# Where the softmax sums and their spread reciprocals are turned: TensorE matmuls before, VectorE 32x32 block turns after

## The chip, the core and the metric

The kernel runs on one core of a Trainium2 chip. A core has five engines with a queue of instructions each: PE (TensorE, matrix products; its weight loads are shown as PEld), DVE (VectorE), ACT (ScalarE), POOL (GpSimd) and SP (SyncE, which here only issues DMAs). The metric is the device time of one launch in microseconds (us), as the median of several runs. The profile is of one execution of its own.

## The reference, cut to what matters

Two independent heads read separate inputs, and their outputs are put side by side. Head A is a long convolution (a state space kernel `K` from complex exponentials, then an FFT convolution of length 4096 over 448 channels). Head B is plain attention over 2048 positions with 16 heads of 28 columns:

```
qkv = (x @ wqkv) ...           # B_x [1, 2048, 448]
scores = einsum("bhqd,bhkd->bhqk", q, k) * 28 ** -0.5
p = softmax(scores, axis=-1)
o = einsum("bhqk,bhkd->bhqd", p, v)
b = o.transpose(...).reshape(B, S, D) @ wo
out = concatenate([a, b], axis=-1)
```

The change lies in the division of the softmax: `o` is computed without it, and each column of `o` is then multiplied by the reciprocal of its row sum.

## The kernel before, in words

**Stages.** The first 228 us or so prepare both heads (projections, seeds of the exponentials). Then comes the attention, with most of head A laid into its gaps. The attention works by *units*: 4 groups `g` of 4 heads times 4 chunks `c` of 512 queries, 16 units numbered 0 to 15. A unit has 16 steps, one for each 128 keys, so the main loop (lines 1061 to 1118) has 256 steps `s`. Units 0 to 11 end while the powers of head A are still being formed on POOL and DVE; the last of these belong to step 200 or so. After that come the spectra and the final products of head A.

**One step.** The order of the instructions is written out by hand, and on each engine the instructions run in the order in which the program issues them (line 919):

```
ORDER = ('m0', 's0', 'm1', 's1', 'v', 'f', 'pv', 'f', 'v', 'k', 'm2', 's2', 'm3', 's3', 'v')
```

- `s0` to `s3` (`s_mm`, line 769): the scores of one head, a PE product into the PSUM tile `pss`, then ACT's exponential `p`.
- `m0` to `m3` (`max_mm`, line 189): part of the row maxima of a unit 19 steps ahead. Each takes a PSUM tile `pm`. `m0` is read by ACT (`rl`), `m1` by DVE (`rl`, which also waits for ACT's `rl`), `m2` and `m3` by DVE reductions (`mx`). From step 237 on there is none of these.
- `v` (`vec`, line 1056): one DVE piece of head A's powers (`g`, `zg`), if any is queued.
- `pv` (`pv_step`, line 776): the products of `p` and `v` into the PSUM tile `po`, summed over the 16 steps. A column of ones stands at index 28 (`DH`) of each head's 32 columns of `v`, so row 28 of each 32 rows of `po` holds the softmax sum.
- `f`: a *slot* (`slot`, line 1012). It runs at most one piece: the queue `urgent` first, then the output projections `p_due`, then `m_due` (three PE pieces for each block of head A), then `u_due` (its FFT pieces, until about step 100), then the spectra and final products (`f_slot`). From step 238 on there is a third slot at the end of each step (line 1109). After the last step, slots follow one another until nothing is left (line 1122).

**The ring.** The pieces and the maxima take their PSUM tile by `w_tile` (line 127): three tiles in turn, whoever asks. Whoever asks for the fourth waits until the readers of the first are done. From about step 200 on it is four tiles of one name.

**The end of a unit** (`fin`, line 789). It is called right after the unit's last `pv`. ACT copies `po` to SBUF as `o` (128 rows: 4 heads of 32; 512 queries). Two closures are queued:

- `sums`, two slots later: 16 small PE products (each is two matmul records in the trace) pick the four sums of each query out of `o` with the constant `sel`, and lay them with the queries on the partitions, 16 columns for each partition. DVE takes the reciprocal `r`, ACT spreads it over 32 columns each (`rb`, 128x512).
- `scale`, four slots after the unit's end: 16 PE products turn `rb` back with `ident`, and DVE multiplies: `on = o * pm`. For groups 0 to 2 `on` goes to DRAM. For the last group, units 12 to 15, four projections (`project`, line 815) follow, of 16 PE products each, whose first 12 read the stored groups (`og`) and whose last 4 read `on`.

Both closures ask the ring for a tile, and both use up a slot of `urgent`, so that the slot's other queues move on by one slot. Head A's final products (`one`, line 901) use a constant `wb`, which `finish` loads when the first of them is due.

Of the kernel before, what the change touches and what calls it, by code (L numbers as in the profile page):

```python
# [8 lines left out]
F32 = mybir.dt.float32  # L9
# [9 lines left out]
D = 448  # L19
# [73 lines left out]
def body(ctx, tc, a, out):  # L93
# [23 lines left out]
    const = pool(ctx, "const")  # L117
    ident = const.tile([128, 128], F32, name="ident")
    nc.sync.dma_start(ident, a["ident"])
    sel = const.tile([128, HG], F32, name="sel")  # L120
    kones = const.tile([128, 1], F32, name="kones")
    w1 = const.tile([128, 2, 128], F32, name="w1")

# [3 lines left out]
    def w_tile():  # L127

        n_ring[0] += 1
        return ps_w[0].tile([128, CQ], F32, name=f"pm{n_ring[0] % ps_w[1]}")  # L130
# [7 lines left out]
    def mm32(o, w, x_, start, stop, at=0):  # L138

        for i in range(w.shape[-1] // 32):  # L140
            c = slice(32 * i, 32 * i + 32)
            nc.tensor.matmul(o[c], w[:, c], x_, start=start, stop=stop, tile_position=(0, at + 32 * i))
# [85 lines left out]
    with ExitStack() as st:  # L228
# [89 lines left out]
        pw2 = s_p.tile([128, LV], F32, name="pw2")  # L318
        nc.sync.dma_start(pw2, a["pw2"])
        nc.sync.dma_start(kones, a["kones"])  # L320
        nc.sync.dma_start(sel, a["sel"])
        nc.sync.dma_start(w1, a["w1"])
        def split_w(s):
            for k in range(NCK):
# [464 lines left out]
    def fin(u, s_):  # L789
        g, c = divmod(u, NQ)  # L790
        o = kq_p.tile([128, CQ], F32, name="o")
        nc.scalar.activation(o, o_u[u], AF.Copy)
        on = kq_p.tile([128, CQ], F32, name="on", bufs=2)
        rb = kq_p.tile([128, 4, HG, 32], F32, name="rb")
        og = og_u.pop(u, None)

        def sums():
            pw = w_tile()
            for t in range(4):
                mm32(pw[:, t * HG:(t + 1) * HG], o[:, t * 128:(t + 1) * 128], sel, start=True, stop=True)  # L800
            r = kq_p.tile([128, 4, HG], F32, name="r", bufs=2)
            nc.vector.reciprocal(r, pw[:, :4 * HG].rearrange("p (t h) -> p t h", h=HG))
            nc.scalar.activation(rb, r[:, :, :, None].to_broadcast([128, 4, HG, 32]), AF.Copy)

        def scale():
            pw = w_tile()
            for t in range(4):
                mm32(pw[:, t * 128:(t + 1) * 128], rb[:, t].rearrange("p h e -> p (h e)"), ident, True, True)
            nc.vector.tensor_tensor(on, o, pw, ALU.mult)
            if g < G - 1:  # L810
                nc.sync.dma_start(on_d[c][g], on)
            else:
                p_due.extend((s_ + PD + PS * t, lambda t=t: project(t)) for t in range(4))

        def project(t):
            pw = w_tile()
            ts = slice(t * 128, (t + 1) * 128)
            for g2 in range(G):
                mm32(pw[:, :D], og[:, g2, ts] if g2 < G - 1 else on[:, ts], wo_t[g2 // 2][:, g2 % 2, :],
                     start=g2 == 0, stop=g2 == G - 1)  # L820
            y = kq_p.tile([128, D], F32, name="y", bufs=2)
            nc.scalar.activation(y, pw[:, :D], AF.Copy)
            q0 = c * CQ + t * 128
            nc.sync.dma_start(out[q0:q0 + 128, D:], y)

        soon_slot(UG[1], sums)
        soon_slot(UG[2], scale)

    fk = {}

# [43 lines left out]
    def finish(f, qc, p, ps, bufs=(2, 2)):  # L874

        t_ = {}

        def rows(t, m, i, n):

            w = t.ap[0][0]  # L880
            return bass.AP(tensor=t.tensor, offset=t.offset + (16 * m + 4 * qc + i) * w + f * DF,
                           ap=[[32 * w, 64], [w, n], [1, DF]])

        def load():
            t_["zi"] = p.tile([128, 4, 2, DF], F32, name="zi", bufs=bufs[0])
            nc.sync.dma_start(t_["zi"], z_d[f].rearrange("(q m h c) k d -> (h c k) q m d", m=2, h=2, c=2)
                              [:, qc * 4:qc * 4 + 4])
            t_["u"] = p.tile([128, 4, DF], F32, name="ut", bufs=2)
            for m in range(2):
                nc.sync.dma_start(t_["u"][64 * m:64 * m + 64], rows(u_a, m, 0, 4))  # L890
            if "dsk" not in fk:
                fk["dsk"], fk["wb"] = p.tile([128, D], F32, name="dsk"), p.tile([128, 64], F32, name="wb")
                t = a["A_D_skip"]
                nc.sync.dma_start(fk["dsk"], bass.AP(tensor=t.tensor, offset=t.offset, ap=[[0, 128], [1, D]]))
                nc.sync.dma_start(fk["wb"], a["wb"])

        def skip():
            nc.gpsimd.tensor_tensor(t_["u"], t_["u"],
                                    fk["dsk"][:, None, f * DF:(f + 1) * DF].to_broadcast([128, 4, DF]), ALU.mult)

        def one(i):
            if i == 0:
                t_["ot"] = p.tile([128, 4, DF], F32, name="ot", bufs=bufs[1])
            pf = ps()[:, :DF]
            for m in range(2):
                mm32(pf[64 * m:64 * m + 64, :], fk["wb"], t_["zi"][:, i, m, :], True, True, 64 * m)
            ot = t_["ot"]
            jbi = lambda t, o_: t.rearrange(o_ + " -> p j b i", j=4, i=2)
            nc.vector.tensor_tensor(jbi(ot[:, i], "p (j b i)"), jbi(pf, "p (b j i)"), jbi(t_["u"][:, i], "p (j b i)"), ALU.add)
            if i % 2:  # L910
                for m in range(2):
                    nc.sync.dma_start(rows(out, m, i - 1, 2), ot[64 * m:64 * m + 64, i - 1:i + 1])
        return load, [(0, lambda i=i: one(i)) for i in range(4)], skip
# [11 lines left out]
    k_seeds(0)  # L925
    k_seeds(0)

    urgent, back = collections.deque(), collections.deque()
    powers = {"g": collections.deque(), "e": collections.deque()}
    done = {"mm": -1}  # L930
    u_jobs = [u_stage1(q) for q in range(16)] + [u_stage2(m) for m in range(16)]
# [73 lines left out]
    def soon_slot(gap, f):  # L1005
        n_urgent[0] += 1
        urgent.append((n_slot[0] + gap, n_urgent[0], f))
        q = sorted(urgent)
        urgent.clear()
        urgent.extend(q)  # L1010

    def slot(s_):
        n_slot[0] += 1
        if urgent and urgent[0][0] <= n_slot[0]:
            urgent.popleft()[2]()
        elif s_ >= NS and f_slot(s_, "s"):
            pass
        elif p_due and p_due[0][0] <= s_:
            p_due.popleft()[1]()
        elif m_due and m_due[0][0] <= s_:  # L1020
            m_due.popleft()[1]()
        elif u_due and u_due[0][0] <= s_:
            u_part(*u_due.popleft()[1:])
        else:
            f_slot(s_, "s") or f_slot(s_, "f")
# [93 lines left out]
    pv_step(*prev)  # L1119
    fin(prev[0], NS)  # L1120
    s = NS
    while urgent or p_due or m_due or u_due or any(q[k] for q in (f_jobs, f_tasks, f_loaded) for k in "sf"):
        slot(s)
        s += 0.5
    assert not k_due and not powers["g"] and not powers["e"]
# [4 lines left out]
def constants():  # L1130
    import numpy as np
    k = {}
    k["ident"] = np.eye(128)
    sel, ones = np.zeros((128, HG)), np.zeros((128, 1))
    for j in range(HG):
        sel[32 * j + DH, j] = 1.0
        ones[32 * j + DH:32 * j + DH + 2] = 1.0
    k["sel"], k["kones"] = sel, ones
    k["pw2"] = np.tile(2.0 ** np.arange(LV), (128, 1))
    n1, k1 = np.arange(N1), np.arange(N1)  # L1140
    n2, k2 = np.arange(N2), np.arange(N2)
    th = 2 * np.pi * np.outer(n1, k1 + 0.25) / N1
    w1 = np.zeros((2, 128, 128))
    wb = np.zeros((2, 2, N1, 2, N1))
    for j in range(4):
        w1[0, 32 * j:32 * j + 32, 32 * j:32 * j + 32] = np.cos(th)
        w1[1, 32 * j:32 * j + 32, 32 * j:32 * j + 32] = np.sin(th)
    for h in range(2):
        wb[h, 0, :, h, :] = np.cos(th).T / L
        wb[h, 1, :, h, :] = np.sin(th).T / L  # L1150
    k["w1"] = w1.transpose(1, 0, 2)
    k["wb"] = wb.transpose(0, 1, 2, 4, 3).reshape(128, N2)
    ph = 2 * np.pi * ((k1[:, None, None] + 0.25) * n2[None, :, None] / L + n2[None, :, None] * k2[None, None, :] / N2)
    c, s = np.cos(ph).transpose(1, 0, 2), np.sin(ph).transpose(1, 0, 2)
    m2 = np.zeros((2, N2, N1, 2, 64))
    m2[0, :, :, 0], m2[0, :, :, 1] = c, s
    m2[1, :, :, 0], m2[1, :, :, 1] = -s, c
    k["m2u"] = m2.reshape(2, 16, 4, N1, 128).transpose(1, 0, 2, 3, 4).reshape(128, N1, 128)
    wa = np.zeros((2, 64, N1, N2, 2))
    ct, st = c.transpose(2, 1, 0), s.transpose(2, 1, 0)  # L1160
    wa[0, ..., 0], wa[0, ..., 1] = ct, -st
    wa[1, ..., 0], wa[1, ..., 1] = st, ct

    wa = wa.reshape(2, 64, N1, 2, 2, 16, 2).transpose(0, 1, 2, 5, 4, 3, 6)
    k["mw"] = np.concatenate([m2.reshape(128, N1, 128), wa.reshape(128, N1, 128)], -1)
    return {n: v.astype(np.float32) for n, v in k.items()}
# [18 lines left out]
```

## Time and profile before

| | us |
|---|---|
| median of 3 runs | 1278.66 (1276.97 to 1278.90) |
| profiled execution, its own time | 1278.83 |
| span of that execution, first to last instruction | 1277.0 |
| PE busy | 1216.2 (95%) |
| ACT busy | 967.0 (76%) |
| DVE busy | 922.6 (72%) |
| POOL busy | 843.6 (66%) |

A row of the profile's groups reads: line, engine, operation, output tile <- input tiles, shapes, number of instructions | total busy us, mean ns of one | idle time of that engine just before them and what ended it. Line 77 is the helper that records every instruction, so groups are told apart by the names of the tiles. In a timeline a row is: start in us, length in us, engine, line, operation, tiles, number of instructions merged, and in brackets the idle time before it with its releaser. DVE records that follow one another overlap by some 0.08 us, so the distance of two starts is a little less than a length.

### The profile page before, as it was taken

What the parts mean: (1) busy time and instruction counts of PE and PEld (TensorE: products, weight loads), DVE (VectorE), ACT (ScalarE), POOL (GpSimd) and SP (SyncE); (2) the same over time, 40 slices, a digit from 0 to 9 for tenths busy, and PEclk for the clock granted to TensorE, in tenths of its full rate; (3) what the DMA queues carried; (4) which work ended last, traced back from release to release, by engine and by line L of the source; (5) the groups of instructions that cost most, each with busy time, mean ns of one, the idle gap of its engine ahead of it and who ended that gap; (6) DMA issues with size and microseconds to landing.
All of it is one profiled execution on the core that took longest, in us unless ns stands there. A gap on an engine that the chain in (4) does not pass through costs nothing.

```text
span 1277.0 us, 33251 instructions
## 1 busy us (share of the span) xinstructions
PE 1216.2 (95%) x12593; PEld 692.5 (54%) x12593; DVE 922.6 (72%) x2106; ACT 967.0 (76%) x2162; POOL 843.6 (66%) x728
## 2 busy tenths in 40 slices
PE   6788888999999999999999999999999999999998
PEld 4666764555555555555555555555555555544433
DVE  5788966877777877778778988888887645645111
ACT  5888865788888888888888888888887656656552
POOL 2666740798788888878689999989995222324321
PEclk9999898899999999999999999999999999999999
DMA  6678789436554645475533133432224533657656
GB/s 194 211 258 290 275 278 359 124 88 187 159 154 114 169 118 159 123 224 177 171 101 96 57 80 105 145 91 71 83 60 149 171 139 135 205 162 237 203 163 174
DMA packets 203528, 206.22 MB, mean 161 GB/s; under 512 B 98344, under 2 KB 162408, under 8 KB 201320
## 3 DMA queue, kind: packets, MB, share of 16 engines
q1 hardware_dynamic: 202840, 203.50, 51.8%
q8 instruction: 99, 1.62, 0.5%
q10 hardware_dynamic: 528, 0.59, 0.2%
q14 instruction: 61, 0.50, 0.1%
HBM read 121.60 MB, written 82.18 MB: 160 GB/s over the span
## 4 chain that ended last, share of the span: by engine, by line
PE 79%; DVE 9%; ACT 5%; issue 3%; POOL 2%; DMA 1%; SPq 1%; ACTq 0%; POOLq 0%; DVEq 0%
PE pm L77 44%; PE pss L77 17%; PE po L77 17%; DVE tri L77 1%; ACT tri L77 1%; DVE mx L77 1%; DVE sg L77 1%; SPq L77 1%; ACT rl L77 1%; DVE hl L77 1%; DVE px L77 1%; ACT p L77 1%; PE pt L77 1%; POOL p L77 1%; DVE g L77 1%
## 5 line engine op out<-in xcount | busy, mean ns | idle before, releaser
L77 ACT ACTIVATE p<-pss 128x512 f32<-128x512 f32 x1024 | 561.3, 611 | 111.5 <-PE pss L77 108.4
L77 PE MATMUL pss<-qhat,khat 128*128 128x512 f32 x1024 | 402.8, 399 | 1.5 <-ACT p L77 1.4
L77 DVE TENSOR_REDUCE mx<-pm 128x1 f32<-128x512 f32 x480 | 308.3, 683 | 108.9 <-PE pm L77 106.8
L77 PE MATMUL pm<-khat,qhat 128*128 128x512 f32 x749 | 326.3, 439 | 6.6 <-ACT rl L77 4.4
L77 POOL TENSOR_TENSOR e<-e,sdb 128x256 f32<-128x256 f32 x168 | 201.8, 1201 | 111.4 <-ACT e L77 62.2
L77 PE MATMUL po<-p,v 128*32 128x512 f32 x2048 | 269.1, 594 | 0.0
L77 POOL TENSOR_TENSOR e<-e,eu 128x256 f32<-128x256 f32 x168 | 248.1, 1477 | 13.2
L77 PEld LDWEIGHTS pm<-khat,qhat 128*128 128x128 f32 x749 | 141.2, 189 | 202.8 <-ACT p L77 46.9
L77 DVE CUSTOM_DVE_ANT_0 rl<-pm,rl 128x512 f32<-128x512 f32 x259 | 178.2, 688 | 73.7 <-ACT rl L77 70.8
L77 PEld LDWEIGHTS pss<-qhat,khat 128*128 128x128 f32 x1024 | 190.4, 188 | 46.1 <-issue 10.8
L77 POOL TENSOR_TENSOR eu<-e,sdb 128x256 f32<-128x256 f32 x168 | 201.9, 1202 | 0.0
L77 POOL TENSOR_TENSOR p<-pr,pr 64x448 f32<-64x448 f32 x64 | 73.1, 1142 | 161.4 <-PE pm L77 134.7
L77 ACT ACTIVATE rl<-pm 128x512 f32<-128x512 f32 x259 | 156.8, 607 | 15.4 <-PE pm L77 9.4
L77 DVE TENSOR_TENSOR g<-g,zg 128x128 f32<-128x128 f32 x392 | 161.9, 413 | 3.4
L77 PE MATMUL pm<-kdif,qhat 128*128 128x512 f32 x249 | 100.9, 405 | 6.0 <-DVE xn L77 4.1
L77 PE MATMUL pm<-xh,khat 128*128 128x512 f32 x256 | 85.0, 423 | 12.1 <-DVE hl L77 5.3
L77 DVE TENSOR_TENSOR zg<-g,zg 128x128 f32<-128x128 f32 x224 | 88.0, 393 | 5.0
L77 PEld LDWEIGHTS pm<-e,g 128*32 128x32 f32 x3584 | 57.2, 109 | 43.9 <-issue 16.2
L77 DVE TENSOR_TENSOR pr<-pm,ub 128x448 f32<-128x448 f32 x64 | 37.0, 619 | 56.4 <-PE pm L77 42.0
L77 PE MATMUL pm<-e,g 128*32 128x64 f32 x3584 | 73.0, 222 | 1.9 <-POOL e L77 1.3
L77 ACT ACTIVATE y<-pm 128x448 f32<-128x448 f32 x48 | 26.5, 553 | 58.2 <-PE pm L77 35.9
L77 ACT ACTIVATE ub<-pm 128x224 f32<-128x224 f32 (+1 forms) x96 | 38.7, 448 | 39.5 <-PE pm L77 37.4
(135 smaller groups left out, 1436.7 us busy)
## 6 DMA issues: line engine op xcount, KB each, us to landing
sdb<-sd SPq DMA_DIRECT2D x55, 336.0 KB
qhat<-q SPq DMA_DIRECT2D x64, 256.0 KB
khat<-k SPq DMA_DIRECT2D x64, 256.0 KB
sd<-sg SPq DMA_DIRECT2D x8, 1456.0 KB
k<-hl SPq DMA_DIRECT2D x16, 512.0 KB
mw<-in_mw SPq DMA_DIRECT2D x16, 512.0 KB
sd<-qhat SPq DMA_DIRECT2D x8, 896.0 KB
yu_d<-ub SPq DMA_DIRECT2D x64, 112.0 KB
```

What stands on the lines that cost most here:

```text
L77: i = f(*args, **kw)
```

## The change

In `sums`, DVE turns `o` in blocks of 32x32 into a tile of the same size as `rb` was, so that the sum of query 32 b + q stands on partition q of its head's 32 rows, in column `DH` of block b; DVE then takes the reciprocal of these 16 columns. In `scale`, DVE turns the reciprocals, each repeated 32 times by a step of zero, into the PSUM tile, which lays them along the free axis again on all 32 rows of the head; then it multiplies as before. The PE products of both closures and ACT's `rb` go. `sums` no longer asks the ring for a tile; `scale` still does.

Both closures leave `urgent` for a new queue `free`. A slot first runs what is due in `free` (two and four slots after the unit's end, as before) and then its own piece, so these closures no longer use up a slot. The constant `sel` goes; `wb` is loaded at the start in its place and no longer by `finish`.

```diff
-    sel = const.tile([128, HG], F32, name="sel")
+    wb = const.tile([128, N2], F32, name="wb")
...
-        nc.sync.dma_start(sel, a["sel"])
+        nc.sync.dma_start(wb, a["wb"])
...
         on = kq_p.tile([128, CQ], F32, name="on", bufs=2)
-        rb = kq_p.tile([128, 4, HG, 32], F32, name="rb")
         og = og_u.pop(u, None)
+        t_ = {}
 
         def sums():
-            pw = w_tile()
-            for t in range(4):
-                mm32(pw[:, t * HG:(t + 1) * HG], o[:, t * 128:(t + 1) * 128], sel, start=True, stop=True)
-            r = kq_p.tile([128, 4, HG], F32, name="r", bufs=2)
-            nc.vector.reciprocal(r, pw[:, :4 * HG].rearrange("p (t h) -> p t h", h=HG))
-            nc.scalar.activation(rb, r[:, :, :, None].to_broadcast([128, 4, HG, 32]), AF.Copy)
+            t = kq_p.tile([128, NK, 32], F32, name="rb")
+            nc.vector.transpose(t.rearrange("p b e -> p (b e)"), o)
+            t_["r"] = kq_p.tile([128, NK], F32, name="r", bufs=2)
+            nc.vector.reciprocal(t_["r"], t[:, :, DH])
 
         def scale():
             pw = w_tile()
-            for t in range(4):
-                mm32(pw[:, t * 128:(t + 1) * 128], rb[:, t].rearrange("p h e -> p (h e)"), ident, True, True)
+            nc.vector.transpose(pw.rearrange("p (b e) -> p b e", e=32), t_["r"][:, :, None].to_broadcast([128, NK, 32]))
             nc.vector.tensor_tensor(on, o, pw, ALU.mult)
...
-        soon_slot(UG[1], sums)
-        soon_slot(UG[2], scale)
+        free.append((n_slot[0] + UG[1], sums))
+        free.append((n_slot[0] + UG[2], scale))
...
-                fk["dsk"], fk["wb"] = p.tile([128, D], F32, name="dsk"), p.tile([128, 64], F32, name="wb")
+                fk["dsk"] = p.tile([128, D], F32, name="dsk")
...
-                nc.sync.dma_start(fk["wb"], a["wb"])
...
     def slot(s_):
         n_slot[0] += 1
+        while free and free[0][0] <= n_slot[0]:
+            free.popleft()[1]()
         if urgent and urgent[0][0] <= n_slot[0]:
             urgent.popleft()[2]()
```

More of the change, by code (lines that the diff above doesn't have):

```diff
@@ L905, in one @@
             for m in range(2):
-                mm32(pf[64 * m:64 * m + 64, :], fk["wb"], t_["zi"][:, i, m, :], True, True, 64 * m)
+                mm32(pf[64 * m:64 * m + 64, :], wb, t_["zi"][:, i, m, :], True, True, 64 * m)
             ot = t_["ot"]
@@ L926, in body @@
     k_seeds(0)
-    urgent, back = collections.deque(), collections.deque()
+    urgent, free = collections.deque(), collections.deque()
     powers = {"g": collections.deque(), "e": collections.deque()}
@@ L1121, in body @@
     s = NS
-    while urgent or p_due or m_due or u_due or any(q[k] for q in (f_jobs, f_tasks, f_loaded) for k in "sf"):
+    while urgent or free or p_due or m_due or u_due or any(q[k] for q in (f_jobs, f_tasks, f_loaded) for k in "sf"):
         slot(s)
@@ L1133, in constants @@
     k["ident"] = np.eye(128)
-    sel, ones = np.zeros((128, HG)), np.zeros((128, 1))
+    ones = np.zeros((128, 1))
     for j in range(HG):
-        sel[32 * j + DH, j] = 1.0
         ones[32 * j + DH:32 * j + DH + 2] = 1.0
-    k["sel"], k["kones"] = sel, ones
+    k["kones"] = ones
     k["pw2"] = np.tile(2.0 ** np.arange(LV), (128, 1))
```

## The prediction

> **What bounds the kernel now.** I read the page first (busy shares, the chain), then busy time by stretch, then what DVE waited for, then the timelines around the ends of the units.
>
> ```profile
> PE 1216.2 (95%) x12593; PEld 692.5 (54%) x12593; DVE 922.6 (72%) x2106; ACT 967.0 (76%) x2162; POOL 843.6 (66%) x728
> PE 79%; DVE 9%; ACT 5%; issue 3%; POOL 2%; DMA 1%; SPq 1%; ACTq 0%; POOLq 0%; DVEq 0%
> ```
>
> The chain that ended last is 79% PE. By stretch (columns: PE, PEld, DVE, ACT, POOL busy), from the end of unit 0 to that of unit 6, of 11, of 13, of 15, and the tail:
>
> ```profile
> 293.00:678.00 385.00, 381.71 (x4550) 210.15 (x4547) 302.74 (x717) 321.35 (x747) 313.15 (x247) 1.00 0.53 152
> 678.00:963.00 285.00, 283.98 (x3445) 162.13 (x3444) 249.66 (x599) 241.32 (x547) 266.89 (x211) 1.00 0.30 86
> 963.00:1105.00 142.00, 141.19 (x1473) 76.03 (x1471) 88.06 (x184) 96.14 (x192) 44.60 (x37) 1.00 0.48 162
> 1105.00:1254.00 149.00, 144.78 (x1499) 66.27 (x1496) 52.59 (x111) 86.74 (x166) 51.18 (x39) 1.00 0.66 200
> 1254.00:1277.00 23.00, 16.98 (x253) 7.07 (x249) 4.05 (x10) 3.40 (x6) 2.18 (x2) 0.96 0.43 114
> ```
>
> PE is nearly always busy. But from 678 to 963 DVE is busy too, 249.66 of 285 us (88%), and the rest of it is short waits. Over 293 to 963 the waits of DVE are:
>
> ```profile
> DVE mx L77 <- PE pm L77: 61.4, 79, 2.1
> DVE rl L77 <- ACT rl L77: 42.0, 113, 1.0
> ```
>
> That is 103 us over 176 steps, 0.59 us a step. After 963 DVE has room: 88 of 142 and 53 of 149 us.
>
> **The change, part by part.** The operations that go or stay:
>
> ```profile
> L77 PE MATMUL pm<-sel,o 128*32 128x4 f32 x512 | 7.0, 175 | 0.3 <-ACT o L77 0.3
> L77 PE MATMUL pm<-ident,rb 128*32 128x128 f32 x512 | 17.3, 275 | 0.6 <-ACT rb L77 0.6
> L77 ACT ACTIVATE rb<-r 128x512 f32<-128x512 f32 x16 | 10.1, 630 | 4.9 <-DVE r L77 4.9
> L77 DVE RECIPROCAL r<-pm 128x16 f32<-128x16 f32 x16 | 4.0, 251 | 0.3 <-PE pm L77 0.3
> L77 DVE TENSOR_TENSOR on<-o,pm 128x512 f32<-128x512 f32 x16 | 10.9, 682 | 2.3 <-PE pm L77 2.1
> ```
>
> *PE.* The products overlap, so I count from start to start. Here is the end of unit 9, PE:
>
> ```profile
> 850.66 0.43 PE L77 MATMUL pm<-sel,o 128*32 128x4 f32 x32
> 850.93 1.06 PE L77 MATMUL po<-p,v 128*32 128x512 f32 x8
> 851.92 0.50 PE L77 MATMUL pm<-khat,qhat 128*128 128x512 f32 x1
> ...
> 853.42 0.41 PE L77 MATMUL pm<-khat,qhat 128*128 128x512 f32 x1
> ...
> 854.22 1.08 PE L77 MATMUL pm<-ident,rb 128*32 128x128 f32 x32
> 855.12 1.04 PE L77 MATMUL po<-p,v 128*32 128x512 f32 x8
> ```
>
> `sums` occupies PE for 850.93 - 850.66 = 0.27 us and `scale` for 855.12 - 854.22 = 0.90 us: 1.17 us a unit, 18.7 us in all. That slots come free changes the order of the other pieces, not their amount.
>
> *ACT* loses 0.63 us a unit. It isn't the bound, so I count nothing.
>
> *DVE.* The reciprocal stays (16 columns, 0.25 us), and so does `on`. Two turns of 512 columns are new. No turn is in this trace. Bounds: the fastest row of DVE by column is a scalar operation between SBUF tiles, 782 ns at best for 1232 columns, which scales to 0.33 us for 512. The slowest reading is that of the same row disturbed, 1627 ns, 2.08 times; twice a usual 512-column operation is 1.4 us.
>
> ```profile
> L77 DVE TENSOR_SCALAR tri<-tri x8: 782/796/1627, 27.2 to 160.4; 128x1232 f32<-128x1232 f32 x8
> ```
>
> I take 0.68 us, the length of `on`, the nearest row in shape; with an allowance of 0.04 us until the next instruction, which needs its result, 0.72. DVE thus gets 1.44 us more a unit.
>
> A rule speaks against this value. The Trainium skill, "VectorE: DVE Perf Modes", section "The three transpose paths", gives 311 ns for a VectorE turn of 128x128 in bf16 and names SBUF as where it goes. Four times 311 ns would be an estimate of 1.24 us a turn; the sum by it stands with the second rival. No run so far shows a turn, into PSUM or into SBUF.
>
> *What lies behind the turns on DVE.* The turn of `sums` stands between two `v` pieces, ahead of the reductions `mx` of `m2` and `m3`. The ring has three tiles: the next step's `m1` takes the tile of `m2`, and its slot that of `m3`. PE issues `m1` 853.42 - 851.92 = 1.50 us after `m2`. DVE in unit 9:
>
> ```profile
> 852.13 0.25 DVE L77 RECIPROCAL r<-pm 128x16 f32<-128x16 f32 x1
> 852.30 0.38 DVE L77 TENSOR_TENSOR g<-g,zg 128x256 f32<-128x256 f32 x1
> 852.59 1.28 DVE L77 TENSOR_REDUCE mx<-pm 128x1 f32<-128x512 f32 x2
> ...
> 855.69 0.68 DVE L77 TENSOR_TENSOR on<-o,pm 128x512 f32<-128x512 f32 x1
> ...
> 857.07 1.29 DVE L77 TENSOR_REDUCE mx<-pm 128x1 f32<-128x512 f32 x2 [0.36 <-PE pm L77]
> ...
> 858.98 0.69 DVE L77 CUSTOM_DVE_ANT_0 rl<-pm,rl 128x512 f32<-128x512 f32 x1 [0.29 <-ACT rl L77]
> ```
>
> `mx` of `m2` ends at 852.59 + 0.6 = 853.2 (the two take 1.28) and `m1` starts at 853.42: 0.2 us of slack. With the turn, `mx` moves by 0.72 and PE stands still for about 0.5 before `m1`, more than the 0.27 it saved. In the scale step the second turn adds 0.72 again. The tile is now held from the turn to the end of `on`, and `m3`, two askers later, waits for it. DVE gets back only its own idle time, 0.36 + 0.29. So unit 9 **loses** 1.44 - 0.65 = 0.8 us; PE's 1.17 are gone. A light end is unit 7:
>
> ```profile
> 738.30 1.29 DVE L77 TENSOR_REDUCE mx<-pm 128x1 f32<-128x512 f32 x2 [0.25 <-PE pm L77]
> ...
> 740.57 0.69 DVE L77 CUSTOM_DVE_ANT_0 rl<-pm,rl 128x512 f32<-128x512 f32 x1 [0.98 <-ACT rl L77]
> ...
> 743.02 1.29 DVE L77 TENSOR_REDUCE mx<-pm 128x1 f32<-128x512 f32 x2 [1.02 <-PE pm L77]
> ```
>
> Here 2.25 us of idle time take the 1.44, and what is left, 0.8 us, is a gain, of which I count 0.65 since `m3` still waits for `on`. The twelve ends of units 0 to 11 lie between these two. By the mean idle time, 0.59 us a step over the 2.5 steps that the two turns reach, 1.47 us stand against 1.44. I take **0** for the twelve together, -8 if all were like unit 7 and +10 if all were like unit 9.
>
> *Units 12 to 14.* DVE has room, so PE's saving counts, except that in the scale step the slot's own piece now takes the tile of `m0`, which ACT still reads. In unit 13:
>
> ```profile
> 1111.40 1.08 PE L77 MATMUL pm<-ident,rb 128*32 128x128 f32 x32
> ...
> 1111.80 0.69 DVE L77 CUSTOM_DVE_ANT_0 rl<-pm,rl 128x512 f32<-128x512 f32 x1 [0.61 <-ACT rl L77]
> ...
> 1112.30 1.04 PE L77 MATMUL po<-p,v 128*32 128x512 f32 x8
> ```
>
> DVE's `rl` waited 0.61 us for ACT's, until 1111.80, 0.4 us after the slot began. So 1.17 - 0.4 = 0.8 each for units 12 and 13, and 1.1 for unit 14, which has no maxima beside it: **-2.7 us**.
>
> *The tail.* Written out by the rules of the queues, three of head A's final products (those with `wb`) move from behind the last unit to steps before it, and one instead of three is left behind the last projection.
>
> ```profile
> 1254.40 0.60 ACT L77 ACTIVATE o<-po 128x512 f32<-128x512 f32 x1 [1.14 <-PE po L77]
> ...
> 1256.54 1.08 PE L77 MATMUL pm<-ident,rb 128*32 128x128 f32 x32 [0.63 <-ACT rb L77]
> ...
> 1257.43 2.44 PE L77 MATMUL pm<-ua,og 128*32 128x448 f32 x24
> ...
> 1257.76 0.69 DVE L77 TENSOR_TENSOR on<-o,pm 128x512 f32<-128x512 f32 x1 [1.41 <-PE pm L77]
> ...
> 1270.60 1.32 PE L77 MATMUL pm<-zi,wb 128*32 128x224 f32 x24
> ...
> 1271.89 2.59 SPq L77 DMA_DIRECT2D out<-ot  x4
> ```
>
> After: `o` is there at 1255.0; turn, reciprocal, turn, `on` give 1255.2 + 0.72 + 0.25 + 0.72 + 0.68 = 1257.6 (1258.45 before). The first projection need not wait for `ident` on PE; its stored part (2.44 us long, 2.25 to the next start) runs meanwhile, and its last part starts at 1257.65 instead of 1257.43 + 2.25 = 1259.7: the projections end 2.0 us earlier. Behind them one product and two output DMAs (0.65 us each to issue) stand instead of three and four: 1.5 us. That is **-3.5 us**; the three products cost some 0.3 us each where they go, **+0.9**.
>
> *Loads.* `wb` comes at the start instead of `sel`, and no `wb` later on SP. The number of DMAs stays, `wb` has 64 columns where `sel` had 4. Only `w1` stands behind it in this group on SP, and the attention is the first to need that, so the loads of the first stage cover it; without that cover it would cost what the longer transfer takes at the start. I count nothing.
>
> **Sum:** 0 - 2.7 - 3.5 + 0.9 = -5.3 us. The profiled execution took 1278.83 us (1.8 around its span of 1277.0), which lies 0.17 above the median: **1273.5 us**.
>
> **The rivals.**
>
> 1. *PE's saving counts in full*: the stalls I see at `m1` and `m3` don't come, because DVE catches up or the turn is short. Fifteen units at 1.17 are 17.6, with the tail's 2.6 it gives 1258.6. For it: PE carries 79% of the chain. Against it: the 0.2 us of slack in unit 9. A turn of 0.33 us alone (2 x 0.35 less in twelve units, at most 8.4) would give 1265. Chance 0.13.
> 2. *Slower: the turn costs more than I take*, on DVE ahead of `mx`, in units 0 to 11. Each 0.1 us of a turn costs 24 x 0.1 = 2.4 us there, so from 0.68 + 0.22 = 0.90 us a turn the change loses. At 1.4 us it gives 1273.5 + 17 = 1290. One mechanism that could do it is in the row of `tri` above: an SBUF to SBUF operation took 1627 instead of 782 ns, beside a busy POOL, and POOL is busy 267 of 285 us in units 7 to 11. By the skill's estimate of 1.24 us the sum would be 1273.5 + 24 x 0.56 = 1287. Against it: the `g` in unit 9, beside the same POOL, keeps its 0.38 us. Chance 0.22.
> 3. *No change*: the heavy ends outweigh the light ones (+4 instead of 0), and the time lies at 1276.5 to 1281. Chance 0.15. That the turns do not give the layout that `on` needs, I hold for less than 0.01.
>
> A rule beside the second rival: the Trainium skill, "SBUF — State Buffer", section "Who interferes with whom", says that DVE operations in two-port modes, or with two SBUF inputs, and POOL shut each other out for a whole instruction. The disturbed `tri` row agrees. Whether a turn is such an operation no run here shows.
>
> **How the numbers follow.** Forecast 0.50 (1268 to 1276.5), rivals 0.13, 0.22, 0.15. A measurement of this kernel can tell about 0.2%, 2.6 us, from no change. Faster by more, below 1276.1: 0.13 + 0.45 = 0.58. Slower by more, above 1281.2: 0.22 and a little of the third. Same: 0.19. The range leaves out most of rival 1 and the upper part of rival 2: 1264 to 1286.
>
> **What would show it.** A turn of 0.6 to 0.75 us in DVE's rows, in both places; PE's `pm` waiting for `on` and `mx` at the ends of units 1, 2, 6 and 9 and those units no shorter than now; units 13 to 15 shorter by about 1 us; the first projection of the tail starting before `on`. Wrong if a turn is far from 0.68 us, or if PE's starts at `m1` and `m3` do not move with DVE.

## The result, and the profile after

The changed kernel takes 1280.01 us (median of 20 runs, 1278.86 to 1281.18); the kernel before, on the same chip, 1278.22 (20 runs, 1276.90 to 1279.59). The ratio of after to before is 1.0015, 95% interval 1.0009 to 1.0021: no gain where 5 us had been forecast, and if anything a small loss. The profiled span is 1278.9 us, 1.9 more than before.

From the page of after, the busy row and the chain of work that ended last:

```profile
PE 1199.8 (94%) x11569; PEld 669.9 (52%) x11569; DVE 942.6 (74%) x2138; ACT 959.2 (75%) x2146; POOL 843.5 (66%) x728
PE 72%; DVE 13%; POOL 5%; ACT 4%; issue 3%; DMA 2%; ACTq 0%; SPq 0%; POOLq 0%; DVEq 0%
```

PE lost its 16.4 us of work and DVE got 20 more, as meant. But the time didn't follow, and in the chain POOL went from 2% to 5%. From the groups of after by shape, what the change added:

```profile
L77 DVE STREAM_TRANSPOSE pm<-r 128x512 f32<-128x512 f32 x16 | 11.5, 720 | 0.0
L77 DVE STREAM_TRANSPOSE rb<-o 128x512 f32<-128x512 f32 x16 | 11.3, 705 | 1.1 <-ACT o L77 1.1
L77 DVE TENSOR_TENSOR on<-o,pm 128x512 f32<-128x512 f32 x16 | 11.0, 687 | 0.5
L77 DVE RECIPROCAL r<-rb 128x16 f32<-128x16 f32 x16 | 4.1, 254 | 0.6
```

A turn takes 0.705 us into SBUF and 0.720 us into PSUM. So a turn is about as long as was assumed, and the loss has to be looked for elsewhere. To find the place, the run is cut at ACT's copy `o<-po`, which marks the end of each unit. The table gives, for the stretch that follows the end of each unit, how much longer it is in after than in before (first column: everything up to the end of unit 0; last column: from the end of unit 15 to the end of the span).

| start | 0 | 1 | 2 | 3 | 4 | 5 | 6 | 7 | 8 | 9 | 10 | 11 | 12 | 13 | 14 | tail |
|---|---|---|---|---|---|---|---|---|---|---|---|---|---|---|---|---|
| -0.6 | -0.8 | +0.1 | +0.4 | -0.2 | -0.5 | -0.3 | +0.4 | -0.8 | 0.0 | +0.7 | 0.0 | **+9.2** | -1.2 | -0.1 | -1.3 | -3.3 |

Without one stretch after would be 7.3 us faster. Its two ends, in ACT's timeline (start, length), first in before, then in after:

```profile
962.59 0.74 ACT L77 ACTIVATE o<-po 128x512 f32<-128x512 f32 x1
...
1028.32 0.60 ACT L77 ACTIVATE o<-po 128x512 f32<-128x512 f32 x1
```

```profile
961.09 0.71 ACT L77 ACTIVATE o<-po 128x512 f32<-128x512 f32 x1
...
1036.03 0.60 ACT L77 ACTIVATE o<-po 128x512 f32<-128x512 f32 x1
```

65.73 us became 74.94. What PE did in the middle of it, before and after:

```profile
981.64 0.65 PE L77 MATMUL pm<-e,g 128*32 128x64 f32 x32
982.08 1.07 PE L77 MATMUL po<-p,v 128*32 128x512 f32 x8
...
983.84 0.50 PE L77 MATMUL pm<-khat,qhat 128*128 128x512 f32 x1
```

```profile
980.57 0.40 PE L77 MATMUL pss<-qhat,khat 128*128 128x512 f32 x1
987.42 1.08 PE L77 MATMUL pm<-e,g 128*32 128x64 f32 x32 [6.46 <-POOL e L77]
988.27 1.94 PE L77 MATMUL po<-p,v 128*32 128x512 f32 x8
...
991.54 0.50 PE L77 MATMUL pm<-khat,qhat 128*128 128x512 f32 x1
```

PE stands for 6.46 us: the next product of head A needs `e`, and POOL hasn't written it. After the wait the same products run slowly: from `pm<-e,g` to the next maxima product 991.54 - 987.42 = 4.12 us instead of 983.84 - 981.64 = 2.20. The windows of after (columns: length, then PE, PEld, DVE, ACT, POOL busy, granted clock, DMA share, GB/s) say why:

```profile
980.00:987.40 7.40, 0.96 (x5) 0.44 (x3) 1.37 (x4) 2.23 (x5) 7.21 (x4) 0.81 0.00 0
987.40:992.00 4.60, 4.58 (x58) 2.26 (x59) 0.00 (x0) 0.53 (x2) 0.00 (x0) 0.57 0.00 0
```

The granted clock is 0.57 in the 4.6 us after the wait. Wait and clock together make 6.46 + 1.92 = 8.4 of the 9.2 us. Why `e` was late stands in POOL's timeline, before and then after:

```profile
963.59 1.30 POOL L77 TENSOR_TENSOR e<-e,eu 128x512 f32<-128x512 f32 x1
964.97 1.91 POOL L77 TENSOR_TENSOR e<-e,sdb 128x1024 f32<-128x1024 f32 x1
...
968.83 2.40 POOL L77 TENSOR_TENSOR e<-e,eu 128x1024 f32<-128x1024 f32 x1
980.11 4.80 POOL L77 TENSOR_TENSOR p<-pr,pr 64x448 f32<-64x448 f32 x4 [8.88 <-PE pm L77]
```

```profile
962.12 1.31 POOL L77 TENSOR_TENSOR e<-e,eu 128x512 f32<-128x512 f32 x1
976.35 4.77 POOL L77 TENSOR_TENSOR p<-pr,pr 64x448 f32<-64x448 f32 x4 [12.93 <-DVE pr L77]
981.20 1.91 POOL L77 TENSOR_TENSOR e<-e,sdb 128x1024 f32<-128x1024 f32 x1
...
985.05 2.32 POOL L77 TENSOR_TENSOR e<-e,eu 128x1024 f32<-128x1024 f32 x1
```

The order of POOL's queue has changed. Before, the three 128x1024 pieces of `e` (and `eu`) came first, and the four joins `p<-pr,pr` of the first spectrum piece after them. In after the joins stand ahead. They wait 12.93 us for DVE's `pr`, and the pieces of `e`, which could have run at 963.5, stand behind them until 981.2.

**The theory.** The closures `sums` and `scale` of unit 11 no longer use up slots. The first spectrum job is loaded at the same place in both kernels: the load of `mw` stands on SP 964.26 - 962.59 = 1.67 us after `o<-po` in before and 962.74 - 961.09 = 1.65 us in after.

```profile
964.26 0.43 SPq L77 DMA_DIRECT2D mw<-in_mw  x1
```

```profile
962.74 0.43 SPq L77 DMA_DIRECT2D mw<-in_mw  x1
```

Its pieces are due two steps later, and there the slots decide. In before, `scale` takes the first slot of that step (PE from 968.26), a power product `pm<-e,g` the second (970.02), and the spectrum waits for the next step. In after, the power product has the first slot (966.87) and the first spectrum piece `pm<-yk,mw` the second. In PE's rows, before and then after, `po<-p,v` lies between the two slots of a step:

```profile
973.94 0.94 PE L77 MATMUL pm<-yk,mw 128*32 128x224 f32 x16
...
977.75 0.96 PE L77 MATMUL pm<-yk,mw 128*32 128x224 f32 x16
978.53 1.04 PE L77 MATMUL po<-p,v 128*32 128x512 f32 x8
```

```profile
968.75 0.96 PE L77 MATMUL pm<-yk,mw 128*32 128x224 f32 x16 [0.37 <-DVE pm L77]
...
973.19 1.04 PE L77 MATMUL po<-p,v 128*32 128x512 f32 x8
974.05 0.94 PE L77 MATMUL pm<-yk,mw 128*32 128x224 f32 x16
```

Counted from the end of unit 11, the first of these pieces starts 968.75 - 961.09 = 7.7 us after it instead of 973.94 - 962.59 = 11.4: one step. The second piece, which also issues the joins, moves up by one slot: from the first slot of a step in before to the second slot of the step before that in after. Between these two slots lies the `k` place (see the order of one step), where the last three pieces of `e` are issued, so the joins now pass them. **The rival** is that the turns themselves, as extra load on DVE, make the loss, and the stall is only where it shows.

### The profile page after: what moved, and what is told of

Read it like the earlier page. It is cut to its first block, busy times and chain, and to the rows that moved or that the text cites. A ratio compares the mean times of both kernels' runs of the same rounds, so it can differ in the third digit from the quotient of the medians.

```text
span 1278.9 us, 31211 instructions
## 1 busy us (share of the span) xinstructions
PE 1199.8 (94%) x11569; PEld 669.9 (52%) x11569; DVE 942.6 (74%) x2138; ACT 959.2 (75%) x2146; POOL 843.5 (66%) x728
## 4 chain that ended last, share of the span: by engine, by line
PE 72%; DVE 13%; POOL 5%; ACT 4%; issue 3%; DMA 2%; ACTq 0%; SPq 0%; POOLq 0%; DVEq 0%
PE pm L77 40%; PE pss L77 15%; PE po L77 15%; DVE mx L77 2%; DVE tri L77 2%; ACT rl L77 1%; ACT p L77 1%; DVE rl L77 1%; POOL qhat L77 1%; DVE g L77 1%; DVE zg L77 1%; POOL p L77 1%; DMA xn<-in_B_x 1%; POOL e L77 1%; PE pt L77 1%
## 5 line engine op out<-in xcount | busy, mean ns | idle before, releaser
L77 PEld LDWEIGHTS pss<-qhat,khat 128*128 128x128 f32 x1024 | 190.4, 188 | 45.5 <-issue 11.4
```

Of the source, the lines that this page charges most:

```text
L77: i = f(*args, **kw)
```

## The experiments

Each gives the median of its runs and the ratio to the kernel before, whose runs were taken beside its own. That kernel took 1278.30 us beside the first four and 1278.25 beside the last three.

**First spectrum piece one step later.** After, with the first spectrum job due one step later; all else as in after.

```diff
-        f_loaded[kind].append((max(f_ready.get((kind, f), 0), s_ + FL[kind]), tasks))
+        f_loaded[kind].append((max(f_ready.get((kind, f), 0), s_ + FL[kind] + ((kind, f, i) == ("s", 0, 0))), tasks))
```

> The changed kernel, but the first spectrum may start one step later, so that its joins on POOL again stand behind the last three e pieces of block 54, as before the change. Theory (a join that moved ahead of e pieces in POOL's queue stalls PE once, at unit 12): the 6.5 us wait of PE for POOL e and the 2 us of slow clock after it go, unit 12 is shorter by 9 us, and the kernel takes 1270 to 1272 us. Rival 1 (the turns on DVE make unit 12 long, by whatever way): no change against the changed kernel, 1280 us. Rival 2 (the loss is spread, the wait only shifts time): 1276 to 1280 us.

Measured: 1269.93 us, ratio 0.9938 (0.9924 to 0.9953). The profile, with a span of 1270.1 us, is of the slowest of the four runs (1271.90 us; the others took 1269.90 to 1269.94). POOL in this kernel:

```profile
967.71 2.37 POOL L77 TENSOR_TENSOR e<-e,eu 128x1024 f32<-128x1024 f32 x1
978.92 4.80 POOL L77 TENSOR_TENSOR p<-pr,pr 64x448 f32<-64x448 f32 x4 [8.84 <-PE pm L77]
```

The order of before is back, PE's wait is gone, and the stretch after unit 11 is 0.1 us shorter than in before instead of 9.2 longer. With both turns in place the kernel is 8.4 us faster than before: the turns aren't the loss.

**The queue alone.** Before's products and ACT's `rb`, but in the new queue.

```diff
-        soon_slot(UG[1], sums)
-        soon_slot(UG[2], scale)
+        free.append((n_slot[0] + UG[1], sums))
+        free.append((n_slot[0] + UG[2], scale))
...
         n_slot[0] += 1
+        while free and free[0][0] <= n_slot[0]:
+            free.popleft()[1]()
```

> The kernel before with its products, but sums and scale go through the new queue that uses up no slot; no turns. Theory (POOL's order): the same stall at unit 12, +8 to +9 us, less 1 to 1.5 us in the tail, where fewer products stand behind the last projection: 1284 to 1287 us. Rival 1 (the turns on DVE are at fault): no stall, 1276 to 1278 us.

Measured: 1288.04 us, ratio 1.0077 (1.0060 to 1.0094), a little above what was expected. The same order on POOL and the same wait on PE, with no turn in the program:

```profile
978.40 4.76 POOL L77 TENSOR_TENSOR p<-pr,pr 64x448 f32<-64x448 f32 x4 [13.34 <-DVE pr L77]
983.25 1.91 POOL L77 TENSOR_TENSOR e<-e,sdb 128x1024 f32<-128x1024 f32 x1
```

```profile
989.47 1.08 PE L77 MATMUL pm<-e,g 128*32 128x64 f32 x32 [6.44 <-POOL e L77]
```

The stretch after unit 11 is 9.9 us longer than in before, all others together 1.0 shorter. So the queue makes the loss, and the rival falls.

**The turns alone.** After, with both closures back in `urgent`, so that they use up slots as before.

```diff
-        free.append((n_slot[0] + UG[1], sums))
-        free.append((n_slot[0] + UG[2], scale))
+        soon_slot(UG[1], sums)
+        soon_slot(UG[2], scale)
```

> The changed kernel with both turns, but sums and scale use up a slot of the urgent queue again, so that the other pieces keep the slots of before. Theory (POOL's order): no stall at unit 12; about 0 over units 0 to 11, -2.7 us over units 12 to 14, -2 us in the tail: 1272 to 1275 us. Rival 1 (the turns are at fault): the stall is there, 1280 us. Rival 2 (DVE's load costs more than PE saves over units 0 to 11): 1277 to 1282 us.

Measured: 1274.60 us, ratio 0.9974 (0.9965 to 0.9983). No stall: the stretch after unit 11 is 0.1 us shorter than in before. The stretches after units 12 to 14 gain 3.2 us. The tail, where 2 us were expected, gains only 0.3, and DVE's timeline of this kernel shows what took them:

```profile
1252.67 0.39 DVE L77 TENSOR_TENSOR ot<-pm,ut 128x224 f32<-128x224 f32 x1 [7.76 <-POOL ut L77]
1252.98 0.70 DVE L77 STREAM_TRANSPOSE rb<-o 128x512 f32<-128x512 f32 x1
```

`o` was there at 1251.36 (ACT's copy starts at 1250.76 and takes 0.60), but the turn stands on DVE behind a piece `ot` that waits for POOL's `ut`, and starts 1.6 us late. PE, which took the sums before, had no such piece ahead of them. In after the same turn starts 0.1 us after `o` is there (1260.26, and 1259.57 + 0.60). With the free slots that `ut` comes sooner: in the first experiment's kernel POOL starts it 4.2 us ahead of the copy of `o` (1246.58 and 1250.75), here 0.2 us ahead (1250.53 and 1250.76). So in the tail the turns need the free slots, which the experiment's expectation had not seen; and with the slots used up, three products of `wb` stay behind the last unit.

**The joins behind `e`.** After, slots untouched; only the joins are put on POOL after the `e` pieces of their step.

```diff
             forth(1)
-            join(0)
-            join(1)
+            joins.append(lambda: (join(0), join(1)))
+            if last_step[0]:
+                joins.popleft()()
...
                 for _ in range(3):
                     if powers["e"]:
                         powers["e"].popleft()()
+                while joins:
+                    joins.popleft()()
```

(`joins` is also emptied at the end of each step; `last_step` holds once the steps are over.)

> The changed kernel with every slot as it is, but the joins of a spectrum are issued on POOL behind the e pieces of the same step. Only POOL's order changes. Theory (POOL's order): like the first run, 1270 to 1272 us. Rival (the earlier start of the spectrum itself, its products or its loads, makes unit 12 long, not POOL's order): 1279 to 1281 us.

Measured: 1271.82 us, ratio 0.9949 (0.9934 to 0.9964). POOL:

```profile
967.60 2.37 POOL L77 TENSOR_TENSOR e<-e,eu 128x1024 f32<-128x1024 f32 x1
976.56 4.79 POOL L77 TENSOR_TENSOR p<-pr,pr 64x448 f32<-64x448 f32 x4 [6.59 <-DVE pr L77]
```

The joins still wait for `pr`, and now nothing that matters stands behind them. The stretch after unit 11 is +0.65 instead of +9.21. The difference, 8.6 us, is the price of the order of seven instructions on POOL; it agrees with the 8.4 us of wait and clock read above. The other 0.65 comes with the earlier slot, and what makes it wasn't traced.

**The turn of the sums twice.** The first experiment's kernel, with the first turn issued twice. This asks what a microsecond on DVE costs, on which the prediction's second rival rests.

```diff
-            nc.vector.transpose(t.rearrange("p b e -> p (b e)"), o)
+            for _ in range(2):
+                nc.vector.transpose(t.rearrange("p b e -> p (b e)"), o)
```

> The first run (later first spectrum), and the turn of the sums is done twice in every unit, the second time over the first with the same result. It measures the price of 0.7 us more on DVE at a unit's end. Theory (over units 0 to 11 DVE stands ahead of the reductions that the ring waits for, with no slack left): +0.4 to +0.7 us at each of the twelve ends, +0.7 in the tail, nothing at units 12 to 14: 1275 to 1279 us. Rival (PE alone is the bound, DVE catches up): +0.7 in the tail alone, 1270 to 1271.5 us.

Measured: 1280.27 us, ratio 1.0015 (1.0005 to 1.0024), somewhat above what was expected. The turns:

```profile
L77 DVE STREAM_TRANSPOSE rb<-o x32: 702/711/715, 296.0 to 1260.4; 128x512 f32<-128x512 f32 x32
```

Against the first experiment's kernel the stretches after units 0 to 11 are 7.8 us longer for twelve turns: 0.65 us for each 0.71, some 0.9 to 1. (By the medians the whole run is 10.3 us longer, by the two profiles 9.0.) It isn't even: almost nothing after units 0 and 4, 1.7 after unit 9, the heaviest end. The tail pays 0.76, and the end of unit 12, which was thought free, 0.82; those of 13 and 14 pay nothing.

**The second turn into SBUF.** The first experiment's kernel; the reciprocals are turned into an SBUF tile, not into the ring's PSUM tile.

```diff
         def scale():
-            pw = w_tile()
+            pw = kq_p.tile([128, CQ], F32, name="rb")
```

> The first run, but scale turns the reciprocals into an SBUF tile instead of a tile of the ring, and on is a product of two SBUF tiles. The ring is not held while DVE turns and multiplies. Theory 1 (the ring's tile held until on costs PE's wait before m3, 0.3 to 0.5 us at most ends): 1266 to 1269 us. Theory 2 (DVE itself is late at these ends, so the ring only shows it): 1269 to 1271 us. Rival (a DVE product of two SBUF tiles is held up beside the busy POOL, as the row of sg, 508 ns usual and 1184 ns at worst, was): on takes up to 1.2 us instead of 0.69 and the kernel 1272 to 1277 us.

Measured: 1278.90 us, ratio 1.0003 (0.9994 to 1.0012), some 9 us slower than the first experiment's kernel with its PSUM tile, and above the ranges of both theories and of the rival. The two rows of DVE in this kernel, and a piece of POOL:

```profile
L77 DVE STREAM_TRANSPOSE rb<-r x16: 702/704/711, 298.8 to 1259.4; 128x512 f32<-128x512 f32 x16
L77 DVE TENSOR_TENSOR on<-o,rb x16: 691/1284/2022, 299.6 to 1260.1; 128x512 f32<-128x512 f32 x16
```

```profile
621.68 2.36 POOL L77 TENSOR_TENSOR eu<-e,sdb 128x1024 f32<-128x1024 f32 x1
```

The turn is no slower and hardly faster, but the product `on` went from 0.687 to a median of 1.28 us, up to 2.02, and the sixteen of them from 11.0 to 19.5 us in all; the POOL piece that lay beside such a product took 2.36 us, where the same piece takes 1.91 in after. The mechanism is the rival's, only larger: the product now has both inputs in SBUF. The Trainium skill, "SBUF — State Buffer", section "Who interferes with whom", says that a DVE instruction with two SBUF inputs contends with a POOL instruction that reads SBUF. These rows agree. What the experiment was also to show, the cost of holding a tile of the ring through both instructions, can't be read from it, since the product itself became longer.

**The heavy ends on PE.** The first experiment's kernel; units 2, 6 and 9, whose stretches became longer in after, end as in before (products, ACT's `rb`, the queue `urgent`); `sel` is loaded again.

```diff
+        if u in (2, 6, 9):
+            soon_slot(UG[1], sums_pe)
+            soon_slot(UG[2], scale_pe)
+        else:
+            free.append((n_slot[0] + UG[1], sums))
+            free.append((n_slot[0] + UG[2], scale))
```

> The first run, but the ends of units 2, 6 and 9, which it made 0.47, 0.37 and 0.66 us longer than before the change, use the products, ACT's spreading and a slot of the urgent queue as before. Theory (what an end gains or loses is set by DVE's idle time around it): these three go back to their old length and nothing else moves, -1.5 us: 1268 to 1269 us. Rival (the slots of later pieces move and give it back elsewhere): 1269.5 to 1272 us.

Measured: 1269.65 us, ratio 0.9929 (0.9916 to 0.9943). The three stretches, +0.5, +0.4 and +0.7 us in the first experiment's kernel, are back to within 0.1 of before; some 0.8 us of this 1.5 is given back after units 4, 8 and 10, and the time lies where the rival put it. Its interval and that of the first experiment overlap, and the two ran beside different runs of before, so it isn't shown that one is better. Both beat before and after.

## Why the prediction was wrong, point by point

**The failed step** is the sentence "That slots come free changes the order of the other pieces, not their amount." It is true, and I counted it at nothing. But the order was what decided: one piece moved up by one slot carried four POOL instructions past three others, at the one place where the rest of the kernel waited for those three. That cost 8.6 us (experiment with the joins behind `e`), more than all gains of the sum together. The tail's pieces I had written out by the rules of the queues, the start of the spectra I had not.

The group of products that waited shows it in one row of after; before, it waited 1.3 us for `e` in all:

```profile
L77 PE MATMUL pm<-e,g 128*32 128x64 f32 x3584 | 73.7, 223 | 10.7 <-POOL e L77 8.2
```

Could it have been seen? In the trace of before the joins start on POOL 8.88 us after the last `e` piece, waiting for PE: any step that carries them up past the `e` pieces puts such a wait in front of work that is ready. That row was there to be asked for.

**A turn** was taken at 0.68 us, and is 0.705 and 0.720: right. The estimate of 1.24 us, made by scaling the 311 ns that the Trainium skill ("VectorE: DVE Perf Modes", "The three transpose paths") gives for 128x128, isn't borne out. The same table names SBUF as the target; here a turn into PSUM works too and costs 15 ns more than one into SBUF. The sixteen turns of `sums` last 701 to 711 ns, and those of units 7 to 10, each of which ran beside a POOL instruction, 703 to 705 ns: POOL doesn't hold up a turn. The second rival falls.

**Ends of units 0 to 10**, counted at 0: measured -0.9 us together (the end of unit 11, without the stall, -0.1 in the first experiment). Light and heavy ends are where they were put. Unit 7: -0.65 forecast, -0.83 measured; unit 9: +0.8 forecast, +0.74 measured; of the ends named as no shorter, 2, 6 and 9 lengthened by 0.4 to 0.7 us, more than any other, and 1 stayed as it was. The forecast waits are there, and one more. After, at the end of unit 9, PE:

```profile
851.78 0.50 PE L77 MATMUL pm<-khat,qhat 128*128 128x512 f32 x1 [0.70 <-DVE mx L77]
...
853.09 0.65 PE L77 MATMUL pm<-e,g 128*32 128x64 f32 x32 [0.57 <-ACT rl L77]
...
855.52 0.50 PE L77 MATMUL pm<-khat,qhat 128*128 128x512 f32 x1 [0.26 <-DVE on L77]
```

PE stands before `m1` for `mx` and before `m3` for `on`. Between them the slot's own piece waits for ACT's `rl`, which the prediction saw for units 12 and 13 alone. DVE at the same place:

```profile
849.86 0.70 DVE L77 STREAM_TRANSPOSE rb<-o 128x512 f32<-128x512 f32 x1
...
851.05 1.27 DVE L77 TENSOR_REDUCE mx<-pm 128x1 f32<-128x512 f32 x2
...
854.78 0.69 DVE L77 TENSOR_TENSOR on<-o,pm 128x512 f32<-128x512 f32 x1
```

That the mean idle time of DVE covers the turns was also right. Its waits in after, over 293 to 963 us:

```profile
DVE mx L77 <- PE pm L77: 52.7, 67, 2.1
DVE rl L77 <- ACT rl L77: 36.7, 106, 0.9
```

They sum to 89 instead of 103 us: 14 us of waiting became work, of the 15.7 that were added there (22 turns at 0.71, those of units 0 to 10). With these two turns the cover is nearly used up: a third one, in `sums`, costs 0.9 us for each us (the turn of the sums twice). The first rival, PE's saving in full, would have needed 14 us from these ends, and falls.

**Units 12 to 14 and the three products of `wb`** that move there: -2.7 + 0.9 = -1.8 forecast, -2.5 measured in after. With the products left behind the last unit (the turns alone) the three ends give -3.2, so the products cost some 0.6. They fall on one stretch: the one after unit 13 is only 0.07 us shorter in after, against 1.15 us with the turns alone. So the stretches don't all become shorter by about 1 us, as the prediction named for a sign.

**The tail**: -3.5 forecast, -3.3 measured. The last part of the first projection starts 1262.79 - 1259.57 = 3.22 us after the start of `o`, where it was 1259.69 - 1254.40 = 5.29: 2.07 us, forecast 2.0. From the last part of the last projection to the end of the span, 1278.9 - 1272.97 = 5.9 us instead of 1277.0 - 1269.85 = 7.15 (the last parts are the rows of `pm<-ua,on`): 1.2, forecast 1.5. PE in the tail of after:

```profile
1262.79 0.96 PE L77 MATMUL pm<-ua,on 128*32 128x448 f32 x8 [0.62 <-DVE on L77]
...
1272.97 0.94 PE L77 MATMUL pm<-ua,on 128*32 128x448 f32 x8
1273.72 0.56 PE L77 MATMUL pm<-zi,wb 128*32 128x224 f32 x8
```

Here PE waits for `on`, which the turns alone show to be fragile: it hangs on no DVE piece standing ahead of the turn.

**Loads**, counted at nothing: the start, up to the end of unit 0, is 0.6 us shorter in after, and 0.1 to 1.4 shorter in the five other kernels that load the same. It varies by that much, and no cost is seen.

**The sum.** Forecast -5.3. Without the one stretch after unit 11, after is at -7.3, and the kernel that takes the stall away and nothing else has a span 6.9 us below that of before (1270.1 and 1277.0; by the medians it is 8.4). So each counted term held within 1 us, and the outcome was decided by the one that wasn't counted. The third rival, no change, came nearest in time (it said 1276.5 to 1281), but by another mechanism: it put the loss on heavy ends all over units 0 to 11, and it is in one place.

## What to carry to other kernels

When a change frees or takes places in an order written out by hand, list for each piece that moves what it issues on every engine, and look at the spot in each in-order queue where it lands: work that waits, put ahead of work that is ready, holds up everything that waits for the latter. The end of one stage and the start of the next is where that costs most, so write the order out there first. And idle time of a busy engine covers an addition only once: ask for the price of the next microsecond as well as for that of the first.

## What the runs showed of the hardware that was not expected

- A DVE turn of 128x512 in fp32, in blocks of 32x32, takes 0.705 us from SBUF to SBUF, and no longer (0.704 us) when its input repeats one value 32 times by a step of zero. With such an input it takes 0.720 us from SBUF to PSUM.
- A DVE product of 128x512 with one input in PSUM takes 0.687 us (686 to 689 ns over 16 of them, 13 beside a POOL instruction); with both in SBUF 0.69 to 2.02 us. In three of the fast ones it was the POOL instruction, started just after, that became longer: `e<-e,eu` at 492.41 took 1.82 us, where the same piece takes 1.30 in after.
- A wait of 6.46 us on PE is paid for twice: in the 4.6 us after it the granted clock was 0.57 (0.50 from 984.57 to 991.39 us, that is from 3.6 us after PE's last product to 4.0 us after its next), the eight products `po<-p,v` took 1.94 us from first start to last end instead of 1.07, and 1.9 us were lost beside the wait itself. The Trainium skill, "TensorE: Matmul & The Clock Gate", section "What's actually happening", says that the clock falls to half after about 3.4 us of idleness and returns after about as long of work; this row agrees.
